# Delta-rule attention and two MoE layers on one core: the first two groups' diagonal Gram blocks are copied from the Gram product, the first join runs in halves, the inverses step by one product

## The chip, the cores and the metric

The kernel runs on one core of a Trainium2 chip. The metric is the device time of one execution in microseconds: 880.42 us, the median of three runs (880.21 to 883.84).

## The reference

Three layers run one after the other, in f32. The first is a delta-rule recurrence for 4 batches of 8 heads, 768 steps, head size 48; the second and third are feed-forward layers over the 3072 tokens that it makes.

```python
for t in range(S):                                   # k_n = k / (|k| + 1e-6)
    y[:, :, t] = einsum('bhd,bhde->bhe', q[:, :, t], state)
    v_old = einsum('bhde,bhd->bhe', state, kt)
    state = state + bt * einsum('bhd,bhe->bhde', kt, vt - v_old)
h = x @ w_in;  e = exp(h - max(h));  solu = h * e / sum(e)        # x: y as (3072, 384)
x = (solu - mean(solu)) / sqrt(var(solu) + 1e-6) * g_ln @ w_out   # d_ff 1024
out = square(relu(x @ w2_in)) @ w2_out                            # d_ff 2048
```

## The kernel before, in words

The recurrence is cut into chunks of 64 steps. Inside a chunk the steps are solved together: the Gram matrix of the chunk's keys, below its diagonal and scaled by beta and the key norms, is inverted, and the chunk's values go through that inverse. A tile `t` (24 in all) holds one pair of chunks of four batch-head pairs on 128 partitions. Its 64x64 Gram matrix is handled as blocks of 32 columns (`HB`): two diagonal blocks, each of which is inverted for itself, and the block between them, with which the two inverses are joined.

Tiles come in groups of four (`G0`): group 0 is t = 0 to 3 (`T1` = 4), group 1 is t = 4 to 7 (`T2` = 8). The stages that the change touches:

- `e_mm(t)` (line 699) multiplies keys by queries and keys into two PSUM banks: 16 f32 products, which are 32 matmul instructions in the profile. `e_out(t)` copies the negated key part to `g` (for the first group to `g0`, which lies in the raw weight buffers `raw[2]` and `raw[3]`), masks the query part into `m`, and sends `g` to the DRAM scratch `gscr`. `load_tb` reads the off-diagonal half back as `g12`.
- `d_tile(t)` (line 779), for the first two groups alone, multiplies the keys a second time, 32 products of 32x32 (64 matmul instructions) a tile, so that the diagonal blocks lie in the PSUM tile `p_h` in the layout that the inversion wants. For later groups the inversion loads them from `gscr`.
- `norms` and `gammas` make the scale `gm` from beta and the norms of the keys (VectorE and GpSimd, then a small matmul, line 867, and ScalarE copies).
- `first` inverts group 0's diagonal blocks on VectorE: a transpose into `tu` (line 1042), four scaled products (1052), 14 steps of a product and a sum on blocks of 16 (1063 and 1074), two more products, two transposes (1101, 1106). `join` then joins the blocks of 16 with small matmuls: `mm1` over all 32 (line 1129), one VectorE operation (1134), then `mm2` and `mm3` in two halves (1151, 1157), and copies into `tr`.
- `turn_in` transposes group 1's diagonal blocks out of `p_h` (line 880), and `inversion(1)` inverts them on GpSimd, row by row: a scaling (916), a triangle (923), and for each of 30 rows a product (948) and a sum (963). From row 10 on the columns are cut in two parts that use two halves of the temporary, so that there are 51 products and 51 sums. Groups 2 to 5 go the same way later.
- `turn(g)` transposes an inverse into the tiles `tr` and `tu` (1214, 1212), after which `prep1`, `prep2` and `z` (1294, 1314, 1341) prepare a tile and the chain of the state (`a_mm`, `o_mm`) takes it.
- `load_w1i` and `load_w1o` bring the weights of the second layer by DMA and convert them on ScalarE and VectorE, with the lower part of `w_out` on GpSimd (437). On VectorE that starts behind `first`'s inverse (`after=first_inv`).

The main loop over `t` runs the chain for tile `t`, `e` for tile `t + 9`, and the second layer for tiles `t - 2` and `t - 3`; the third layer follows.

What sets the order is a planner: every operation is handed to `Plan.add` with an engine, an assumed cost, what it reads and writes, and a priority. `Plan.order` simulates the engines in 12 rounds and emits all operations in the order of the best round; each engine then runs its own in that order. `HOLD` is how long an engine is kept for a more urgent operation that is about to be ready. All DMAs are issued from SP's queue. `gate` makes every DMA that is handed to the planner after it wait, in the plan, for the scratch write of tile 3.

Of the kernel before, what the change touches and what calls it, by code (L numbers as in the profile page):

```python
# [123 lines left out]
class Plan:  # L124
# [11 lines left out]
    HOLD = {"pe": 0.0, "dve": 0.042, "act": 0.174, "pool": 0.0, "sp": 0.0, "x": 0.0}  # L136
# [138 lines left out]
def c_turn(n):  # L275
    return 0.07 + n * 1.95e-3
# [12 lines left out]
def tile_delta_moe_moe(  # L289
# [39 lines left out]
    gscr = [dpool.tile([P, 2, GS * NP, HB], F32, name=f"gscr{g}") for g in range(NG)]  # L329
# [41 lines left out]
    v.tensor_reduce(out=low16, in_=ibd[:, HB // 2 :], axis=AX.X, op=ALU.add, negate=True)  # L371
# [36 lines left out]
    ngm = ap_.tile([P, HB], F32, name="ngm")  # L408
# [17 lines left out]
    pool.memset(tr[:, :, :, HB:], 0.0)  # L426
    g0 = raw_all[:, NRAW - 2 :].bitcast(F32).rearrange("q a n u -> q (a n u)")
    g0 = g0.rearrange("q (t h s c) -> q t h s c", t=4, h=2, s=2 * NP)
# [20 lines left out]
    def load_w(src, n, prio, bank, keep=False):  # L449
# [13 lines left out]
        if src.dtype == F32:  # L463
# [8 lines left out]
            [kr, *(("A", "g0", x) for x in range(4) if kr == ("A", "raw", NRAW - 2 + x // 2))],  # L472
# [187 lines left out]
    def e_in(t):  # L660
        if t < 2:
            return kql_[t], [("A", "kql", t)]
        if 4 <= t < 7:
            x, k = (ez_[t - 4], ("ez", t - 4)) if t < 6 else (junk, ("junk",))
            return x.rearrange("q (i p c) -> q i p c", i=2, p=NP), [k]
        return kqe_[t % 2], [("A", "kqe", t % 2)]

    def e_banks(t):
        if t >= LA:
            return pu, ku  # L670
        return (
            ((p_h[:, 0:512], p_h[:, 512:]), (("h", 0), ("h", 1))),
            ((p_tr, p_x1), (("tr",), ("x1",))),
            (pu, ku),
            ((p_a, p_o), (("A", "a"), ("A", "o"))),
        )[t if t < T1 else (1 + (t - T1) % 2 * 2 if t < T2 else 2)]
# [25 lines left out]

    def e_out(t, prio):
# [7 lines left out]
        if t < T1:  # L711
            gt, kg = g0[:, tg].rearrange("q h (i p) c -> q h i p c", i=2), [("A", "g0", tg)]
        banks, kb = e_banks(t)
        for i in range(2):
            gp, kep = banks[i].rearrange("q (p c) -> q p c", p=NP), [kb[i]]
            add(
                "act",
                c_act(256),
                lambda i=i, gp=gp: act.mul(
                    gt[:, :, i].rearrange("q h p c -> q p h c"),  # L720
                    gp[:, :, C:P].rearrange("q p (h c) -> q p h c", h=2),
                    -1.0,
                ),
                kep,
                kg,
                prio + ev,
            )
# [16 lines left out]
            else:  # L744
# [9 lines left out]
                )  # L754
        return dma(
# [7 lines left out]

    def e_tile(t, prio):
        e_load(t, prio)
        fused(1.15, [e_mm(t)], prio)
        return e_out(t, prio)

    def d_tile(t, prio):
        kq, kkq = e_in(t)  # L770
        d = p_h.rearrange("q (s t c) -> q s t c", t=4, c=HB)[:, :, group(t)[1]]

        def mm():
            for i, p, h in both:
                f = heads[h]
                for e in range(2):
                    o = (h ^ i) * C + e * HB
                    k = kq[f, i, p, C + e * HB : C + e * HB + HB]
                    pe.matmul(d[o : o + HB, i * NP + p], k, k, start=True, stop=True)  # L779

        add("pe", 0.7, mm, [*kkq, *((*kkq[0], "in", h) for h in range(2))], [("h", 0), ("h", 1)], prio)
# [33 lines left out]
    def gammas(g, prio):  # L815
# [55 lines left out]
        if g == 1:  # L871
            add("act", c_act(HB), lambda: act.mul(ngm, gt, -1.0), [kgt], [("ngm",)], prio)

    last_inv = []

    def turn_in():
        add(
            "dve",
            c_turn(HB * HB),
            lambda: v.transpose(it_[1].rearrange("s r c -> s c r"), p_h.rearrange("r (s t c) -> r c t s", t=4, c=HB)),  # L880
            [("h", 0), ("h", 1)],
            [("A", "itr", 1, q) for q in range(4)] + [("A", "it", 1, q) for q in range(2)],
            PR["turn1"],
        )

    def inversion(g, en, prio):
# [3 lines left out]
        it, itmp = it_[g % 2], junk[:, 512:] if g == 1 else itmp_  # L890
        kgm, kic = ("A", "gm", g % 2), ("A", "itc", g % 2)
        kts = [("A", "it", g % 2, q) for q in range(2)]
        ktm = [("A", "itmp", g == 1, q) for q in range(2)]
        kj = [("junk",)] if g == 1 else []
# [16 lines left out]
        gc, kgc = (ngm, [("ngm",)]) if g == 1 else (gm, [kgm])  # L911
        gb = gc.unsqueeze(1).to_broadcast([P, HB, HB])
# [4 lines left out]
            [*kraws, *kgc],  # L917
            [*kts, kic, *kj],
# [18 lines left out]
        s1, half_ = 9, HB * HB // 4  # L937
        used, run, brk = [], 0.0, []
        for j in range(1, HB - 1):
            nr = HB - 1 - j  # L940
            for q, (c0, c1) in enumerate(((0, min(j, s1)), (s1, j))):
                w_ = c1 - c0
                if w_ <= 0:
                    continue
                tm = itmp[:, q * half_ : q * half_ + nr * w_].rearrange("p (r s) -> p r s", r=nr)
                mul = one(
                    nr * w_,
                    lambda tm=tm, j=j, nr=nr, w_=w_, c0=c0, c1=c1: eng.tensor_tensor(  # L948
                        out=tm,
                        in0=it[:, j + 1 :, j : j + 1].to_broadcast([P, nr, w_]),  # L950
                        in1=it[:, j : j + 1, c0:c1].to_broadcast([P, nr, w_]),
                        op=ALU.mult,
                    ),
                    [kts[q], kic],
                    [ktm[q]],
                    brk,
                    full=False,
                )
                if q == 0:
                    used = [*used[-1:], mul]  # L960
                last = one(
                    nr * w_,
                    lambda tm=tm, j=j, c0=c0, c1=c1: eng.tensor_tensor(  # L963
                        out=it[:, j + 1 :, c0:c1],
                        in0=it[:, j + 1 :, c0:c1],
                        in1=tm,
                        op=ALU.add,
                    ),
                    [ktm[q], *kj],
                    [kts[q]],  # L970
                    used[:-1] if q else (),
                )
                run += 2 * c_pool(nr * w_)
                if g == 1 and run > 0.75:

                    fn = lambda: pool.memset(idle, 0.0)
                    brk = [add("pool", 0.1, fn, (), [("idle",)], prio, after=[last])]
                    run = 0.0
# [16 lines left out]
    def first(prio):  # L995
# [3 lines left out]
        it, kit = it_[0], [("A", "it", 0, q) for q in range(2)]  # L999
        kgs = [("A", "kqe", 0), ("A", "kqe", 0, "in", 0), ("A", "kqe", 0, "in", 1)]  # L1000
        gs = kqe_[0].rearrange("q i p c -> q (i p c)").rearrange("q (s c) -> q s c", c=HB)
        kh = [("h", 0), ("h", 1)]
        x = xo.rearrange("q a b -> q (a b)")[:, 0:512].rearrange("q (b r c) -> q b r c", b=2, r=H2)
        kx = [("xo", c) for c in range(3)]
# [5 lines left out]
        def dve(n, fn, r, w, c=None):  # L1010
            return add("dve", c or c_dve(n) + 0.09, fn, r, w, prio)
# [6 lines left out]
                in_=gm.unsqueeze(1).to_broadcast([P, HB, HB]),  # L1018
# [3 lines left out]
                compare_op=ALU.is_gt,  # L1022
# [7 lines left out]
        add(  # L1030
            "act",
            c_act(HB * HB),
            lambda: act.copy(
                gs.rearrange("q (t s) c -> q s t c", t=4), p_h.rearrange("q (s t c) -> q s t c", t=4, c=HB)
            ),
            kh,
            kgs,
            prio,
        )
        dve(  # L1040
            0,
            lambda: v.transpose(tu.rearrange("s r c -> s c r"), p_h.rearrange("r (s t c) -> r c t s", t=4, c=HB)),
            kh,
# [3 lines left out]
        for o, ko in ((org, ku[:1]), (x, kx)):  # L1047
            for b in range(2):
# [3 lines left out]
                    lambda o=o, b=b, q=q: v.scalar_tensor_tensor(  # L1052
                        out=o[:, b], in0=tu[:, q, q], scalar=-1.0, in1=it[:, q, q], op0=ALU.mult, op1=ALU.mult
                    ),
                    [*ktu(), *kit],
# [25 lines left out]
        for b in range(2):  # L1081
# [7 lines left out]
                        in1=gm[:, q].unsqueeze(2).to_broadcast([P, H2, H2]),  # L1089
                        op=ALU.mult,  # L1090
                    ),
                    [*kx, kgm],
# [15 lines left out]
        def join():  # L1108

            add(  # L1110
                "pool",
                1.0,
                lambda: pool.tensor_copy(aj[:, :, H2:], ibd[:, H2:].unsqueeze(1).to_broadcast([P, HB, H2])),
                (),
                kit,
# [3 lines left out]
            a1 = p_h[:, 0:512].rearrange("q (s c) -> q s c", c=H2)  # L1119
# [5 lines left out]
            def mm1():  # L1125
                for s in range(HB):
                    for hb in range(4):
                        q, k = slice(hb * HB, hb * HB + HB), slice(hb * HB, hb * HB + H2)
                        pe.matmul(a1[q, s], gs[k, s], td[k, s], start=True, stop=True)

            add("pe", 2.0, mm1, [*kgs, *ktd], [("h", 0)], prio)
            dve(
                512,
                lambda: v.scalar_tensor_tensor(
                    out=aj[:, :, 0:H2],
# [858 lines left out]
```

## Time and profile before

| what | value |
|---|---|
| median of three runs | 880.42 us (880.21 to 883.84) |
| the profiled execution, device time | 886.9 us |
| its span (first to last instruction) | 885.2 us |
| TensorE busy | 808.7 us, 11016 matmuls |
| VectorE busy | 469.8 us |
| ScalarE busy | 448.3 us |
| GpSimd busy | 280.9 us |
| granted TensorE clock over the span | 0.976 of full speed |

The profile is that of one execution, and all durations below are from it. An engine is busy while one of its instructions runs; the idle time before an instruction is put down to what released it ("issue" where the profile shows nothing that the engine waited for). Matmul durations overlap, since matmuls are pipelined. The span begins with a stretch in which the first two groups are prepared, goes on to the main loop, and ends with the third layer.

### The profile page before, as it was taken

What the parts mean: (1) busy time and instruction counts of PE and PEld (TensorE: products, weight loads), DVE (VectorE), ACT (ScalarE), POOL (GpSimd) and SP (SyncE); (2) the same over time, 40 slices, a digit from 0 to 9 for tenths busy, and PEclk for the clock granted to TensorE, in tenths of its full rate; (3) what the DMA queues carried; (4) which work ended last, traced back from release to release, by engine and by line L of the source; (5) the groups of instructions that cost most, each with busy time, mean ns of one, the idle gap of its engine ahead of it and who ended that gap; (6) DMA issues with size and microseconds to landing.
All of it is one profiled execution on the core that took longest, in us unless ns stands there. A gap on an engine that the chain in (4) does not pass through costs nothing.

```text
span 885.2 us, 26110 instructions
## 1 busy us (share of the span) xinstructions
PE 808.7 (91%) x11016; PEld 752.2 (85%) x11016; DVE 469.8 (53%) x906; ACT 448.3 (51%) x1006; POOL 280.9 (32%) x729
## 2 busy tenths in 40 slices
PE   5537689999899999899999999999999999999997
PEld 4436568889787788778788999999999999999997
DVE  5387784564876775865746543343434343343332
ACT  2236686866567658476656444343434333343333
POOL 5387488979569569610000000000000000000000
PEclk9999879999798899999999999999999999999999
DMA  9844664553778465434144312020201002010101
GB/s 205 256 118 143 179 187 141 146 151 108 217 199 253 149 173 170 148 108 157 47 150 134 101 37 55 1 54 0 54 1 45 10 1 55 1 27 0 28 1 27
DMA packets 70053, 89.34 MB, mean 101 GB/s; under 512 B 23088, under 2 KB 54832, under 8 KB 69936
## 3 DMA queue, kind: packets, MB, share of 16 engines
q1 hardware_dynamic: 69936, 87.68, 34.4%
q8 instruction: 86, 1.41, 0.7%
q14 instruction: 31, 0.25, 0.1%
HBM read 65.64 MB, written 22.02 MB: 99 GB/s over the span
## 4 chain that ended last, share of the span: by engine, by line
PE 84%; DVE 4%; issue 4%; ACT 4%; DMA 3%; POOL 0%; SPq 0%; ACTq 0%; POOLq 0%
PE h L1716 22%; PE acc L1760 22%; PE p_h L1451 12%; PE p_x L1573 11%; PE p_u L1341 2%; PE p_a L1368 2%; PE p_u L699 2%; PE p_tr L1553 2%; PE p_o L1399 1%; PE p_a L1314 1%; PE p_a L1398 1%; PE p_a L1294 1%; DMA kqe<-in_kin_dram 1%; PE p_h L779 1%; DVE sc L1466 1%
## 5 line engine op out<-in xcount | busy, mean ns | idle before, releaser
L1737 DVE TENSOR_TENSOR xt<-xt 128x384 f32<-128x384 f32 x128 | 71.5, 559 | 162.5 <-ACT xt L1729 162.4
L1729 ACT ACTIVATE xt<-h 128x384 f32<-128x384 f32 x128 | 63.0, 492 | 166.8 <-PE h L1716 166.6
L1716 PE MATMUL h<-x1h,w2h 128*128 128x384 f32 x384 | 128.5, 335 | 0.8 <-ACT xt L1729 0.8
L1716 PE MATMUL h<-x1l,w2h 128*128 128x384 f32 x384 | 128.3, 334 | 0.0
L1716 PE MATMUL h<-x1h,w2l 128*128 128x384 f32 x384 | 128.3, 334 | 0.0
L1760 PE MATMUL acc<-woh,xh 128*128 128x384 f32 x258 | 86.3, 334 | 0.0
L1760 PE MATMUL acc<-woh,xl 128*128 128x384 f32 x258 | 86.2, 334 | 0.0
L1760 PE MATMUL acc<-wol,xh 128*128 128x384 f32 x258 | 86.2, 334 | 0.0
L1573 PE MATMUL p_x<-zh,wgh 128*128 128x256 f32 x288 | 84.1, 292 | 0.3 <-ACT xo L1587 0.3
L1573 PE MATMUL p_x<-zh,wgl 128*128 128x256 f32 x288 | 81.2, 282 | 0.0
L1573 PE MATMUL p_x<-zl,wgh 128*128 128x256 f32 x288 | 81.2, 282 | 0.0
L963 POOL TENSOR_TENSOR it<-it,itmp 128x85 f32<-128x85 f32 (+29 forms) x204 | 76.2, 399 | 2.4
L948 POOL TENSOR_TENSOR itmp<-it 128x85 f32<-128x85 f32 (+29 forms) x204 | 73.4, 385 | 2.4
L1716 PEld LDWEIGHTS h<-x1h,w2h 128*128 128x128 f32 x384 | 72.1, 188 | 1.1 <-ACT xt L1729 1.1
L1716 PEld LDWEIGHTS h<-x1l,w2h 128*128 128x128 f32 x384 | 72.1, 188 | 0.0
L1716 PEld LDWEIGHTS h<-x1h,w2l 128*128 128x128 f32 x384 | 72.1, 188 | 0.0
L437 DVE TENSOR_TENSOR xl<-xt,xh 128x384 fp32r<-128x384 f32 x86 | 48.0, 558 | 44.9 <-ACT xh L432 44.6
L432 ACT CAST xh<-xt 128x384 fp32r<-128x384 f32 x86 | 44.3, 515 | 46.3 <-DVE xt L1737 45.1
L1451 PE MATMUL p_h<-w1h,xh 128*128 128x512 f32 x144 | 64.0, 445 | 2.8 <-DVE xl L437 2.8
L1451 PE MATMUL p_h<-w1l,xh 128*128 128x512 f32 x144 | 59.7, 415 | 0.0
L1451 PE MATMUL p_h<-w1h,xl 128*128 128x512 f32 x144 | 59.6, 414 | 0.0
L1573 PEld LDWEIGHTS p_x<-zh,wgh 128*128 128x128 f32 x288 | 54.2, 188 | 2.7 <-ACT xo L1587 0.5
(233 smaller groups left out, 1950.1 us busy)
## 6 DMA issues: line engine op xcount, KB each, us to landing
kql<-in_kin_dram SPq DMA_DIRECT2D x22, 512.0 KB, 4.5
kqe<-in_kin_dram SPq DMA_DIRECT2D x38, 192.0 KB, 4.8
raw<-in_w2i_dram SPq DMA_DIRECT2D x12, 512.0 KB, 5.4
raw<-in_w2o_dram SPq DMA_DIRECT2D x16, 384.0 KB, 4.6
gscr<-g SPq DMA_DIRECT2D x20, 256.0 KB, 5.1
m<-in_ktok_dram SPq DMA_DIRECT2D x24, 192.0 KB, 3.8
vt<-in_vtok_dram SPq DMA_DIRECT2D x24, 192.0 KB, 4.5
x1scr<-xo SPq DMA_DIRECT2D x12, 384.0 KB, 2.6
```

The costliest lines, as they stand in the source:

```text
L432: add("act", c_act(n), lambda: act.copy(hi(), src()), r, [w[0]], prio)
L437: lambda: le.tensor_tensor(out=lo(), in0=src(), in1=hi().bitcast(F32), op=ALU.subtract),
L699: pe.matmul(gp[i][rows[h ^ i], p], kq[f, i, p, C:P], kq[f, i, p], start=True, stop=True)
L948: lambda tm=tm, j=j, nr=nr, w_=w_, c0=c0, c1=c1: eng.tensor_tensor(out=tm, in0=it[:, j + 1 :, j : j + 1].to_broadcast([P, nr, w_]), in1=it ...
L963: lambda tm=tm, j=j, c0=c0, c1=c1: eng.tensor_tensor(out=it[:, j + 1 :, c0:c1], in0=it[:, j + 1 :, c0:c1], in1=tm, op=ALU.add,),
L1341: pe.matmul(zp[i][rows[h], p].rearrange("q (j c) -> q j c", j=7), tb[r, i * NP + p], m[r, i, :, p], start=True, stop=True,)
L1451: pe.matmul(p_h[:, sl], xx[:, c], ww[:, c, sl], start=(c == 0 and k == 0), stop=(c == 2 and k == 2),)
L1573: pe.matmul(p_x1[:, 0 : 2 * P], ww[:, f, c * P : c * P + P], zz[:, f], start=(f == 0 and k == 0), stop=(f == 7 and k == 2),)
L1716: pe.matmul(late["h2", ih], late[ww][:, c, s], xx[:, c], start=(c == 0 and k == 0), stop=(c == 2 and k == 2),)
L1729: lambda: act.activation(out=rt, in_=late["h2", ih], func=AF.Relu),
L1737: lambda: v.tensor_tensor(out=gg, in0=rt, in1=rt, op=ALU.mult),
L1760: pe.matmul(late["acc", a], gg[:, a * P : a * P + P], late[ww][:, f], start=(f == 0 and k == 0), stop=(f == 15 and k == 2),)
```

## The change

The diff is cut to its core; what is left out are mostly changed buffer keys, that is, names by which the planner orders reads and writes.

- `d_tile` and `turn_in` are gone. `e_out` for t < 8 makes two ScalarE copies of 128 columns a bank in place of one of 256: one to the place of `g12` (`first_g`), one to the group's array of diagonal blocks `gd_` (in `junk` for group 0, in `raw[3]` for group 1). `own` then copies the odd blocks from the former into the latter, one part on ScalarE, one on GpSimd.
- Group 0 no longer goes through `gscr` in either direction; group 1 writes half as much and reads it back as before.
- `first` reads `gd_[0]`; its four products take `gm` itself, and the triangle comes in at the last products. The copy from `p_h` on ScalarE (line 1033) is gone. Tile 6 takes the buffer `kqe` and not `junk`.
- In `join`, `mm1` and the VectorE operation behind it run in halves, and the block of the identity is copied on ScalarE, not GpSimd.
- In `inversion`, each row is one product and one sum.
- The copy of `vt` to `R` for t = 0 goes to ScalarE; `gate` is no longer set; `HOLD` of GpSimd is 0.11.

```diff
-    HOLD = {... "pool": 0.0, ...}
+    HOLD = {... "pool": 0.11, ...}
...
+    def first_g(t):
+        if t < 2:
+            return g0[:, 2 * NP * t : 2 * NP * t + 2 * NP], ("A", "tb", 0, 0)
+        if t >= T1:
+            return g_[t % 2][:, 1].rearrange("q i p c -> q (i p) c"), ("A", "g", t % 2)
+        return g12_[t % 2], ("A", "g12", t % 2)
...
+            if t < T2:
+                b0, kb0 = first_g(t)
+                s0 = slice(i * NP, i * NP + NP)
+                ss = slice((2 * tg + i) * NP, (2 * tg + i + 1) * NP)
+                for h, to, kg_, ss in ((1, b0, [kb0], s0), (0, gd_[g], kgd_[g], ss)):
+                    add("act", c_act(128),
+                        lambda gp=gp, to=to, ss=ss, h=h: act.mul(to[:, ss], gp[:, :, C + h * HB : C + h * HB + HB], -1.0),
+                        kep, kg_, prio)
...
+    def own(t, prio):
+        g, tg = group(t)
+        b0, kb0 = first_g(t)
+        for h in range(2):
+            q, ss = slice((2 * h + 1) * HB, (2 * h + 2) * HB), slice(2 * NP * tg, 2 * NP * tg + 2 * NP)
+            add("pool" if h else "act", 0.35,
+                lambda q=q, fn=pool.tensor_copy if h else act.copy: fn(gd_[g][q, ss], b0[q]),
+                [kb0], [kgd_[g][h]], prio)
...
-            for q, (c0, c1) in enumerate(((0, min(j, s1)), (s1, j))):
...
+            tm = itmp[:, 0 : nr * j].rearrange("p (r s) -> p r s", r=nr)
+            one(nr * j, lambda ...: eng.tensor_tensor(out=tm,
+                    in0=it[:, j + 1 :, j : j + 1].to_broadcast([P, nr, j]),
+                    in1=it[:, j : j + 1, 0:j].to_broadcast([P, nr, j]), op=ALU.mult), ...)
+            last = one(nr * j, lambda ...: eng.tensor_tensor(
+                    out=it[:, j + 1 :, 0:j], in0=it[:, j + 1 :, 0:j], in1=tm, op=ALU.add), ktm, kts)
...
-        add("act", c_act(HB * HB), lambda: act.copy(gs..., p_h...), kh, kgs, prio)
-            lambda: v.transpose(tu.rearrange("s r c -> s c r"), p_h.rearrange("r (s t c) -> r c t s", t=4, c=HB)),
+            lambda: v.transpose(tu.rearrange("s r c -> s c r"), gs.rearrange("r s c -> r c s")),
...
-            add("pe", 2.0, mm1, [*kgs, *ktd], [("h", 0)], prio)
             for n in range(2):
+                def mm1(n=n):
+                    for s in range(16):
+                        for hb in range(4): ...
+                add("pe", 1.1, mm1, [*kgs, *ktd], [kh[n]], pr)
+                add("dve", c_dve(256) + 0.09, ...)
...
-            fn = lambda: v.tensor_copy(R, vp)
+            fn = lambda: (v.tensor_copy if t else act.copy)(R, vp)
...
     for t in range(T1):
-        d_tile(t, -66 + t)
+        own(t, -62)
     gammas(0, -61)
     join = first(-55)
     for t in range(T1, T2):
         e_tile(t, PR["e0"] + 0.1 * t)
+        own(t, PR["e0"] + 0.1 * t)
         norms(t, PR["n1"])
-    for t in range(T1, T2):
-        d_tile(t, PR["e0"] + 0.5)
-    turn_in()
+    add("dve", c_turn(HB * HB), lambda: v.transpose(it_[1]..., gd_[1]...), kgd_[1], ..., PR["turn1"])
     join()
     gammas(1, -56)
-    gate.append(wr)
     inversion(1, "pool", PR["inv1"])
...
-    load_tb(0, PR["prep0"])
     prep_z(0, PR["prep0"])
-    load_tb(1, PR["prep0"] + 2)
     prep_z(1, PR["prep0"] + 2, (1,))
...
-            if n2:
+            if n2 and t + 2 >= T1:
                 load_tb(t + 2, tp + PR["prep"])
```

## Rows read from the trace of the kernel before

**Rows 1.** Busy time by stretch: microseconds, busy (instructions) by engine, clock, DMA share, GB/s.
```profile
0.00:75.40 75.40, 35.05 (x1488) 30.13 (x1488) 44.04 (x117) 19.91 (x54) 49.08 (x126) 1.00 0.67 179
75.40:126.80 51.40, 39.13 (x866) 31.36 (x866) 39.54 (x81) 38.96 (x101) 31.45 (x98) 0.88 0.68 190
126.80:395.00 268.20, 254.65 (x5114) 220.05 (x5114) 175.46 (x341) 179.99 (x433) 198.00 (x506) 0.95 0.56 163
395.00:885.20 490.20, 479.83 (x3555) 470.64 (x3549) 210.72 (x369) 209.48 (x423) 2.38 (x3) 1.00 0.16 45
```

**Rows 2.** The chain that ended last, in order of time: start, microseconds, what.
```profile
17.65 1.13 PE p_h L779 x72
18.78 1.21 issue
...
21.52 4.66 issue
...
38.72 3.43 issue
...
95.80 4.74 issue
```

**Rows 3.** DMA queue of instructions, whole span: packets, MB, share of 16 engines.
```profile
q8 instruction: 86, 1.41, 0.7%
```

**Rows 4.** Timeline of VectorE: start, microseconds, line, operation, idle before and its releaser.
```profile
20.50 0.41 DVE L748 TENSOR_TENSOR m<-p_u,mask 128x256 f32<-128x256 f32 x1
...
27.86 1.98 DVE L1042 STREAM_TRANSPOSE tu<-p_h 128x1024 f32<-128x1024 f32 x1 [6.39 <-ACT kqe L1033]
...
42.60 1.93 DVE L880 STREAM_TRANSPOSE it<-p_h 128x1024 f32<-128x1024 f32 x1 [8.31 <-PE p_h L779]
...
48.94 2.49 DVE L1386 COPY r<-vt 128x384 f32<-128x384 f32 x1
...
55.44 1.11 DVE L1101 STREAM_TRANSPOSE itmp<-it 128x512 f32<-128x512 f32 x1
```

**Rows 5.** Timeline of TensorE, the join and the first tile behind it.
```profile
56.60 2.95 PE L1129 MATMUL p_h<-itmp,kqe 16*32 16x16 f32 x205 [8.10 <-DVE itmp L1101]
...
62.53 1.28 PE L1151 MATMUL p_u<-it,tu 32*32 32x32 f32 x76 [0.94 <-DVE it L1134]
...
75.42 1.28 PE L1341 MATMUL p_u<-m,tr 64*64 64x112 f32 x11 [0.54 <-ACT tr L1327]
```

**Rows 6.** Timeline of ScalarE: two copies out of PSUM.
```profile
17.95 0.38 ACT L719 ACTIVATE raw<-p_o 128x256 f32<-128x256 f32 x1
...
73.74 0.27 ACT L1300 COPY ys<-p_a 128x128 f32<-128x128 f32 x1 [1.78 <-PE p_a L1294]
```

**Rows 7.** Instructions of line 1386: duration in ns, shortest, median, longest; first and last start.
```profile
L1386 DVE COPY r<-vt x2: 664/1578/2492, 48.9 to 267.0; 128x384 f32<-128x384 f32 x2
```

**Rows 8.** Timeline of GpSimd: inversion of group 1, then rows of a later one.
```profile
48.86 2.35 POOL L916 TENSOR_TENSOR it<-it,ngm 128x1024 f32<-128x1024 f32 x1
...
53.31 0.24 POOL L948 TENSOR_TENSOR junk<-it 128x30 f32<-128x30 f32 x1
...
94.64 1.00 POOL L437 TENSOR_TENSOR wgl<-wst,wgh 128x384 fp32r<-128x384 f32 x1 [11.81 <-ACT wgh L432]
...
118.09 1.92 POOL L988 TENSOR_TENSOR it<-it,gm 128x1024 f32<-128x1024 f32 x1
...
201.30 0.56 POOL L948 TENSOR_TENSOR itmp<-it 128x198 f32<-128x198 f32 x1
201.94 0.78 POOL L963 TENSOR_TENSOR it<-it,itmp 128x198 f32<-128x198 f32 x2
...
208.74 0.83 POOL L948 TENSOR_TENSOR itmp<-it 128x153 f32<-128x153 f32 x2
...
210.31 0.81 POOL L948 TENSOR_TENSOR itmp<-it 128x144 f32<-128x144 f32 x2
```

**Rows 9.** The chain that ended last between 56.6 and 75.4 us, its shares by line.
```profile
by line: issue 37.6%; PE p_u L1151 21.6%; PE p_h L1129 20.7%; PE p_h L1157 5.1%; ACT tr L1171 4.9%; DVE it L1134 4.1%; PE p_a L1294 3.3%; ACT ys L1300 1.4%; ACT tr L1327 1.4%
```

More of the change, by code (lines that the diff above doesn't have):

```diff
@@ L327, in bufs @@
         return [pool_.tile(shape, dt, name=f"{name}_{i}") for i in range(n)]
-    gscr = [dpool.tile([P, 2, GS * NP, HB], F32, name=f"gscr{g}") for g in range(NG)]
+    gscr = [dpool.tile([P, 2, GS * NP, HB], F32, name=f"gscr{g}") for g in range(1, NG)]
+    gscr = [None, *gscr]
     x1scr = [dpool.tile([P, 3, 2 * P], F32, name=f"x1scr{i}") for i in range(NT // 2)]
@@ L471, in load_w @@
             (),
-            [kr, *(("A", "g0", x) for x in range(4) if kr == ("A", "raw", NRAW - 2 + x // 2))],
+            [kr],
             prio - 1,
@@ L767, in e_tile @@
         return e_out(t, prio)
[L769 to L781, printed above, removed]
     def norms(t, prio, after=()):
@@ L935, in inversion @@
         )
-        s1, half_ = 9, HB * HB // 4
-        used, run, brk = [], 0.0, []
+        run, brk = 0.0, []
         for j in range(1, HB - 1):
             nr = HB - 1 - j
-            for q, (c0, c1) in enumerate(((0, min(j, s1)), (s1, j))):
[L942 to L978, printed above, removed]
@@ new lines, in inversion @@
+            tm = itmp[:, 0 : nr * j].rearrange("p (r s) -> p r s", r=nr)
+            one(
+                nr * j,
+                lambda tm=tm, j=j, nr=nr: eng.tensor_tensor(
+                    out=tm,
+                    in0=it[:, j + 1 :, j : j + 1].to_broadcast([P, nr, j]),
+                    in1=it[:, j : j + 1, 0:j].to_broadcast([P, nr, j]),
+                    op=ALU.mult,
+                ),
+                [*kts, kic],
+                ktm,
+                brk,
+                full=False,
+            )
@@ new lines, in inversion @@
+            last = one(
+                nr * j,
+                lambda tm=tm, j=j: eng.tensor_tensor(
+                    out=it[:, j + 1 :, 0:j], in0=it[:, j + 1 :, 0:j], in1=tm, op=ALU.add
+                ),
+                ktm,
+                kts,
+            )
+            run += 2 * c_pool(nr * j)
+            if g == 1 and run > 0.75:
+                fn = lambda: pool.memset(idle, 0.0)
+                brk = [add("pool", 0.1, fn, (), [("idle",)], prio, after=[last])]
+                run = 0.0
@@ L1029, in first @@
         add("pool", 0.3, lambda: pool.memset(it[:, H2:, 0:H2], 0.0), (), kit, prio)
[L1030 to L1039, printed above, removed]
-        dve(
-            0,
-            lambda: v.transpose(tu.rearrange("s r c -> s c r"), p_h.rearrange("r (s t c) -> r c t s", t=4, c=HB)),
-            kh,
+        dve(
+            0,
+            lambda: v.transpose(tu.rearrange("s r c -> s c r"), gs.rearrange("r s c -> r c s")),
+            kgs,
             ktu(),
@@ L1110, in join @@
             add(
-                "pool",
-                1.0,
-                lambda: pool.tensor_copy(aj[:, :, H2:], ibd[:, H2:].unsqueeze(1).to_broadcast([P, HB, H2])),
+                "act",
+                0.55,
+                lambda: act.copy(aj[:, :, H2:], ibd[:, H2:].unsqueeze(1).to_broadcast([P, HB, H2])),
                 (),
-                kit,
+                [kit[1]],
                 prio,
             )
-            a1 = p_h[:, 0:512].rearrange("q (s c) -> q s c", c=H2)
+            a1 = [p_h[:, i * 512 : i * 512 + 256].rearrange("q (s c) -> q s c", c=H2) for i in range(2)]
             f_, k_ = [z.rearrange("q (s c) -> q s c", c=HB) for z in p_u], ku
@@ L1159, in mm3 @@
                             )
[L1161 to L1163 removed]
+                ka = [kit[1], kit[2 + n]]
+                add("pe", 1.1, mm2, [*ktu(hs=[n]), *ka], [k_[n]], pr)
+                add("pe", 0.6, mm3, [*ktu(hs=[n]), *ka], [ku_[n]], pr)
                 sl = slice(2 + 2 * n, 4 + 2 * n)
@@ L1203, in cols @@
             return tr[q, s0 : s0 + 4, :, o : o + HB].rearrange("q t s c -> q (t s) c")
+        if g == 1 and not lower:
+            add(
+                "pool",
+                0.6,
+                lambda: pool.memset(tr[:, 0, :, HB:], 0.0),
+                (),
+                [("A", "tb", 0, k) for k in (*range(5), *kup)],
+                prio - 20,
+            )
         cs = [slice(c, c + HB // 4) for c in range(0, HB, HB // 4)]
@@ L1810, in tile_delta_moe_moe @@
         e_tile(t, PR["e0"] + 0.1 * t)
+        own(t, PR["e0"] + 0.1 * t)
         norms(t, PR["n1"])
-    for t in range(T1, T2):
-        d_tile(t, PR["e0"] + 0.5)
-    turn_in()
+    add(
+        "dve",
+        c_turn(HB * HB),
+        lambda: v.transpose(it_[1].rearrange("s r c -> s c r"), gd_[1].rearrange("r s c -> r c s")),
+        kgd_[1],
+        [("A", "itr", 1, q) for q in range(4)] + [("A", "it", 1, q) for q in range(2)],
+        PR["turn1"],
+    )
     join()
     gammas(1, -56)
-    gate.append(wr)
     inversion(1, "pool", PR["inv1"])
```

173 lines of the change are left out of this document (94 added, 79 removed).

## The prediction

> **What bounds the kernel now.** I read busy time by stretch first [rows 1]. From 395 us on TensorE is busy for 479.83 of 490.20 us, from 126.8 to 395 for 254.65 of 268.20: no edit of the change touches that work, and little idle time is left in it. In the first 75.4 us, though, TensorE is busy for 35.05, VectorE for 44.04, ScalarE for 19.91 and GpSimd for 49.08 us: nothing is full, so a chain of waits sets this stretch, and all that the change edits lies here or feeds tile 4 soon after. What is saved here should come off the end almost whole.
>
> Second, the chain that ended last, in order of time [rows 2]. Its largest pieces in the first 50 us are stalls of TensorE marked "issue", in which it waited for nothing that the profile shows: 1.21 us at 18.78, 4.66 at 21.52, 3.43 at 38.72, all beside the small products of `d_tile`; a later one is 4.74 at 95.80. The queue of instructions moved 1.41 MB in 86 packets [rows 3], that is 16.4 KB a packet; the 11016 matmuls and as many weight loads are 22032 instructions, 256 a packet. I read the stalls as TensorE waiting for its own next packet of 128 matmuls with their loads: where products are tiny, it eats code faster than code comes.
>
> [...]
>
> Third, VectorE's timeline, which carries group 0's inverse [rows 4]. The inverse starts at 27.86, behind 6.39 us of idle time, since `p_h` was finished late. At 42.60 `turn_in`'s transpose stands in the middle of it, having waited 8.31 us for the `d_tile` of group 1, and the inverse's steps queue behind it. At 48.94 a copy to `R` takes 2.49 us. At 55.44 comes the transpose that feeds the join, which TensorE starts at 56.60; tile 0's `z` product follows at 75.42 [rows 5].
>
> **The change part by part.** *The second Gram product goes.* `d_tile` was 8 tiles x 64 = 512 of the 1488 matmuls before 75.4 us, four packets of code. What the inverse now waits for is ScalarE's copies. The last copy of tile 3 ended at 17.95 + 0.38 = 18.33 [rows 6]. A copy of 128 columns was 0.27 us, one of 256 was 0.38 [rows 6], so two small ones for a large one add 0.16 a bank: 0.3 for tile 3's two banks, and about 0.4 for its `own` copies: 19.1. But VectorE is busy with masks and the scale until 20.50 + 0.41 = 20.91 [rows 4]. So the transpose moves from 27.86 to 20.9: **-7.0**. Bounds: 19.1 if VectorE's order leaves a gap (-8.8); 21.5 if all of ScalarE's extra work for the group (8 x 0.16 + 4 x 0.38 = 2.8) and a last hand-over of 0.4 stand in a row (-6.4). `gm` needs the 8 matmuls of line 867; they no longer stand behind `d_tile`, and the first stall came only after tiles 0 to 3 (4 x 32) and 72 of `d_tile`'s [rows 2], 200 matmuls, so the four products find it ready.
>
> *`turn_in`'s wait.* The transpose of group 1 now needs tiles 4 to 7 copied. TensorE has 128 matmuls for them, directly behind the first 136; at most one packet boundary lies in that, so they should be done near 27 us, while VectorE's inverse runs to 35. **-8.3**; if the planner puts the transpose early, some 2 us of the wait stay. Its own 1.93 us stays.
>
> *The copy to `R`.* It took 2.49 us, where its other instance took 0.66 [rows 7], beside GpSimd's scaling of 2.35 at 48.86 [rows 8]; on ScalarE, idle there, it leaves this chain: **-2.5**.
>
> [...]
>
> *The join in halves.* TensorE stood 0.94 us before `mm2` for the VectorE operation [rows 5]. Now the second half of `mm1` can run under the first half's: **-0.9**. If the planner sets `mm2`'s first half directly behind `mm1`'s first, 128 matmuls less stand ahead, 2.95 x 128/205 = 1.8 us more; I don't count on it, since a free TensorE takes what is ready, and that is `mm1`'s second half. The copy of the identity on ScalarE costs nothing while ScalarE is idle; if it isn't, 0.6.
>
> The sum for tile 0: 7.0 + 8.3 + 2.5 + 0.9 = 18.7 us; `z` at 56.7 in place of 75.4.
>
> *Inverses by one product.* In the split form, row 14 (153 + 85 columns) takes 210.31 - 208.74 = 1.57 us [rows 8]; its two products overlap. For one product: 0.24 us at 30 columns, 0.56 at 198 [rows 8], so 1.9 ns a column, 0.64 at 238, and 201.94 - 201.86 = 0.08 between dependent ones; twice that is 1.43. So 0.14 at best in each of 21 rows, less in the short ones: 2 us a group, nothing like the 40% of instructions that go. For groups 2 to 5 it is worth nothing at the end, since TensorE sets that stretch.
>
> *What tile 4 waits for.* Group 1's inversion ran from 48.86 to 118.09 + 1.92, with an idle 11.81 us in it for the weights [rows 8]. Its start was held by `turn_in` like VectorE and gains 7.0 + 8.3 = 15.3, less eight new GpSimd copies (256 columns on 32 partitions; by its products of 0.24 to 0.56 an estimate of 0.4 each, 3.2), plus 2 for its length: 14.1. The 11.8 us of idle time are slack for that, and the wait itself moves with the main chain, 18.7. The end moves between 14.1 and 18.7; I take **17.5** for the whole.
>
> *DMAs.* Group 0's scratch writes (4 x 256 KB), half of group 1's (4 x 128 KB) and two loads of 128 KB go: 1.8 of the 179 GB/s x 75.4 us = 13.5 MB [rows 1]. The weights, no longer gated, may be issued before tiles 6 and 7, whose buffers come free late. The same DMA time without 13% in 57 us is a share of 0.76 where 0.67 was: not full. I cost it at nothing; if code packets queue behind the weights, it is the third rival.
>
> So the profiled execution should go from 886.9 to 869.4 (885.2 span and 1.7 around it). It lies 6.5 above the median of the runs, and I assume the same after: 880.4 - 17.5 = **863 us**.
>
> **The rivals.** *GpSimd becomes the bound at tile 4.* If its masks for tile 7 and the copies of `own` hold it 3 us more, and the single products, each waiting for the one before, save nothing, group 1's inverse gains 15.3 - 3.2 - 3 = 9.1: 871. For it: GpSimd is the busiest engine of the first stretch [rows 1]. Against: the 11.8 us of slack.
>
> *The stalls are not code, or don't go with it.* Then the start and `turn_in` stay put but for the matmuls' own time, and the copy, the join and some 1.5 us are what is left: 2.5 + 0.9 + 1.5 = 5: 875. Against: packets of 256 instructions and stalls that sit in runs of tiny products.
>
> *Code packets wait behind the weights (slower).* In the join, 37.6% of 18.8 us, 7.1 us, are already "issue" [rows 9], over five packets. From the join to 126.8 there are twelve (640 and 866 matmuls). The gain of 17.5 is gone when each waits 1.5 us longer; at 2 more, well under the 4.66 and 4.74 seen, 24 are lost: 887. For it: the gate goes, and the loads get denser. Against: fewer bytes in all, and 0.68 of DMA share in that stretch [rows 1].
>
> *More than counted.* The stall of 4.74 at 95.80 falls elsewhere and the halves give their 1.8: 17.5 + 6.5 = 24: 856.
>
> **How the numbers follow.** The forecast has 0.60 (its own range, by the bounds of its terms, 857 to 869), GpSimd 0.17, stalls that stay 0.08, more than counted 0.08, code behind weights 0.07. A new order of all engines adds some scatter, which I put into the ends: 850 to 877. Half a per cent, 4.4 us, is about what can be told from no change. Only the slower rival lies above 885: slower 0.07; between, 0.05, from a milder form of it and of the stalls that stay; faster 0.88.
>
> **What would show it.** Right: 10504 matmuls; no stall of 3 to 5 us before 30 us; the inverse's transpose near 21; no idle time of several microseconds on VectorE inside the inverse; `mm1` near 38, tile 0's `z` near 57, and the main loop the same shape moved left. Wrong: `z` early but tile 4 late (GpSimd); the join longer than 19 us with more "issue" (code); or a gain that dies after 126.8, which would say that the main loop was not TensorE's.

## The result, and the profile after

The median after is 869.44 us (868.05 to 871.15) against 880.88 before (880.21 to 883.84), four runs each: a ratio of 0.9865, with a 95% interval from 0.9836 to 0.9893, and a gain of 11.4 us. The profiled execution went from 886.9 to 871.15 us, 15.75 less, its span from 885.2 to 869.4. Forecast were 863.0, that is a gain of 17.5, and 869.4 for the profiled execution.

Busy time by stretch of the kernel after (columns as in [rows 1]); the first two stretches end at tile 0's `z` and where [rows 1] end theirs, the last row runs to the end of a stretch used below.

```profile
0.00:61.15 61.15, 29.54 (x1041) 25.70 (x1041) 43.72 (x118) 26.34 (x84) 46.32 (x110) 0.66 0.69 188
61.15:126.80 65.65, 56.82 (x1358) 46.46 (x1352) 51.89 (x105) 53.81 (x134) 47.73 (x104) 0.80 0.72 202
126.80:395.00 268.20, 249.02 (x5005) 216.71 (x5005) 174.90 (x336) 177.50 (x426) 164.60 (x310) 0.96 0.54 161
...
0.00:186.00 186.00, 142.17 (x3402) 121.30 (x3403) 124.75 (x276) 117.03 (x305) 139.34 (x301) 0.80 0.62 170
```

The first stretch is 14.3 us shorter than in [rows 1], with 5.5 us less of TensorE's work. The queue of instructions of the kernel after, four packets fewer than in [rows 3]:

```profile
q8 instruction: 82, 1.34, 0.7%
```

VectorE's timeline of the kernel after, for [rows 4]: the inverse from its transpose (1040) to those that feed the join.

```profile
18.80 1.94 DVE L1040 STREAM_TRANSPOSE tu<-junk 128x1024 f32<-128x1024 f32 x1
...
23.86 0.43 DVE L1050 TENSOR_TENSOR p_u<-tu,gm 128x256 f32<-128x256 f32 x1 [2.67 <-ACT gm L904]
24.21 1.47 DVE L1050 TENSOR_TENSOR xo<-tu,gm 128x256 f32<-128x256 f32 x1
...
37.83 1.07 DVE L1102 STREAM_TRANSPOSE itmp<-it 128x512 f32<-128x512 f32 x1
38.98 2.07 DVE L1831 STREAM_TRANSPOSE it<-raw 128x1024 f32<-128x1024 f32 x1
40.94 1.90 DVE L1107 STREAM_TRANSPOSE tu<-it 128x1024 f32<-128x1024 f32 x1
43.34 0.46 DVE L1140 SCALAR_TENSOR_TENSOR it<-p_h,low,ibd 128x256 f32<-128x256 f32 x1
```

The transpose starts 9.06 us earlier, then stands 2.67 for `gm`; inside the inverse no wait of several microseconds and no copy to `R` are left (line 1401 is on ScalarE, 0.51 us). TensorE's join, for [rows 5] (1134 is `mm1`, 1157 and 1163 `mm2` and `mm3`, 1309 and 1329 `prep1` and `prep2`, 1356 `z`):

```profile
38.95 1.91 PE L1134 MATMUL p_h<-itmp,junk 16*32 16x16 f32 x128 [1.70 <-DVE itmp L1102]
43.94 0.92 PE L1163 MATMUL p_h<-tu,it 32*32 32x32 f32 x53 [3.08 <-DVE it L1140]
...
46.40 0.21 PE L1134 MATMUL p_h<-itmp,junk 16*32 16x16 f32 x1
...
48.17 1.68 PE L1134 MATMUL p_h<-itmp,junk 16*32 16x16 f32 x111 [1.26 <-issue]
...
52.45 0.38 PE L1309 MATMUL p_a<-tr 32*32 32x32 f32 x12 [2.31 <-issue]
...
56.17 0.48 PE L1157 MATMUL p_u<-it,tu 32*32 32x32 f32 x19 [1.80 <-issue]
...
61.15 1.13 PE L1356 MATMUL p_u<-m,tr 64*64 64x112 f32 x12
```

The join starts 17.65 us earlier and takes 22.2 us where it took 18.8. ScalarE's timeline of the kernel after has the copy (`tuc`) that frees `mm1`'s second half:

```profile
45.34 0.35 ACT L1188 COPY itmp<-p_h 128x256 f32<-128x256 f32 x1
```

GpSimd's, for [rows 8]: group 1's inversion (936 to 997), then a row of 238 columns in a later one.

```profile
41.89 2.35 POOL L936 TENSOR_TENSOR it<-it,gm 128x1024 f32<-128x1024 f32 x1
...
92.06 1.91 POOL L997 TENSOR_TENSOR it<-it,gm 128x1024 f32<-128x1024 f32 x1
...
130.15 0.62 POOL L963 TENSOR_TENSOR itmp<-it 128x238 f32<-128x238 f32 x1
130.85 0.65 POOL L976 TENSOR_TENSOR it<-it,itmp 128x238 f32<-128x238 f32 x1
131.58 0.61 POOL L963 TENSOR_TENSOR itmp<-it 128x240 f32<-128x240 f32 x1
```

The chain of waits after, for [rows 2]: in front of the join no "issue" piece above 0.75 us is left; the longest one now is this.

```profile
126.14 3.96 issue
```

### The profile page after: what moved, and what is told of

It is laid out like the page before. It is cut to its first block, busy times and chain, and to the rows that moved or that the text cites. A ratio compares the mean times of both kernels' runs of the same rounds, so it can differ in the third digit from the quotient of the medians.

```text
span 869.4 us, 24895 instructions
## 1 busy us (share of the span) xinstructions
PE 800.3 (92%) x10504; PEld 747.3 (86%) x10504; DVE 469.4 (54%) x906; ACT 453.0 (52%) x1030; POOL 259.5 (30%) x523
## 4 chain that ended last, share of the span: by engine, by line
PE 82%; ACT 5%; DMA 5%; DVE 4%; issue 3%; POOL 1%; SPq 0%; ACTq 0%; DVEq 0%; POOLq 0%
PE h L1731 23%; PE acc L1775 22%; PE p_x L1588 12%; PE p_h L1466 11%; PE p_a L1383 2%; PE p_tr L1568 2%; PE p_u L703 2%; PE p_u L1356 2%; DMA m<-in_ktok_dram 2%; PE p_o L1414 1%; ACT xt L1438 1%; PE p_a L1309 1%; DVE sc L1481 1%; PE p_a L1329 1%; PE p_a L1413 1%
## 5 line engine op out<-in xcount | busy, mean ns | idle before, releaser
L1731 PEld LDWEIGHTS h<-x1h,w2h 128*128 128x128 f32 x384 | 72.1, 188 | 0.0
L976 POOL TENSOR_TENSOR it<-it,itmp 128x30 f32<-128x30 f32 (+14 forms) x120 | 62.6, 521 | 8.5
L963 POOL TENSOR_TENSOR itmp<-it 128x30 f32<-128x30 f32 (+14 forms) x120 | 58.4, 486 | 8.6
```

What stands on the lines that cost most here:

```text
L963: lambda tm=tm, j=j, nr=nr: eng.tensor_tensor(out=tm, in0=it[:, j + 1 :, j : j + 1].to_broadcast([P, nr, j]), in1=it[:, j : j + 1, 0:j].to ...
L976: lambda tm=tm, j=j: eng.tensor_tensor(out=it[:, j + 1 :, 0:j], in0=it[:, j + 1 :, 0:j], in1=tm, op=ALU.add),
L1731: pe.matmul(late["h2", ih], late[ww][:, c, s], xx[:, c], start=(c == 0 and k == 0), stop=(c == 2 and k == 2),)
```

## The experiments

Kernels of one set ran on one chip beside the kernel before, whose medians in the three sets were 879.85, 878.25 and 878.45 us, with single runs from 871.1 to 886.8. Ratios are to before, with 95% intervals.

**Set 1. Is it code?** `b_again` and `a_again` are before and after unchanged. `b_nod` is before without most of the second Gram product:

```diff
                 for e in range(2):
+                    if (i, p, h, e) != (0, 0, 0, 0):
+                        continue
```

`a_all` is after with four moves in the emitted order: group 1's transpose behind the first 1140, group 0's `gm` product ahead of tile 4's `e`, tile 0's `z` ahead of tile 1's `prep1` (with the join's last copy ahead of tile 1's `ys`), the loads of tiles 6 and 7 ahead of the weights.

b_again: 

> The kernel before, unchanged, profiled once more. The first profiled execution took 886.9 us, 6.0 more than the median of the runs. If that was the scatter of one execution (what I hold now), this profile lands near 881 and the difference of some 6 us lies in one stretch that can be named (a stall, a stretch at the lower granted clock). Rival: profiling itself costs 6 us in this kernel, and this one is near 887 again.

b_nod: 

> The kernel before with d_tile cut to 1 of its 32 products a tile (496 matmuls fewer in all); waits, copies and every engine's order stay, and the diagonal blocks are not computed. Theory (the 'issue' stalls are TensorE waiting for code, 128 matmuls a packet): nearly four packets go, VectorE's transpose moves from 27.9 to about 21, its wait of 8.3 before the second transpose goes, tile 0's z comes some 15 us earlier (near 60), time about 866. Rival (the stalls are something else): only the matmuls' own time goes, some 6 us of TensorE and 2 to 3 at the end; stalls of 3 to 5 us before 45 us stay; about 878.

a_again: 

> The changed kernel, unchanged: a better interval and a second profile. Expected 869.4, ratio 0.987; tile 0's z near 61 and the main loop as in the first profile to 1 or 2 us. Rival: the profiled executions of both kernels scatter by some 6 us, then this one may lie anywhere from 866 to 873.

a_all: 

> The changed kernel with its planned order kept but for four moves: turn_in's transpose behind the first half's VectorE operation of the join; group 0's scale matmul ahead of tiles 4 and 5; tile 0's z ahead of tile 1's first two products (with one ScalarE copy); the loads of tiles 6 and 7 ahead of the first weights. Theory (these four places are where the chain lost what I had counted): 2.0 + 2.5 + 1.3 us earlier at tile 0's z, near 55.5, and 4 to 6 us less in all, 864. Rival (the main loop is held by weights, scale and inversion, not by tile 0): z as early, but the time within 1 us of 869.4.

Measured: `b_again` 878.53 us, profiled, `z` at 72.1. So a profile adds nothing like 6 us; the first one of before was a long execution of a kernel that scatters. Of the 8.4 us by which its span is longer, 3.3 had gone by tile 0's `z`, where a stall of 4.66 us was 2.90 in `b_again`, and 6.7 by tile 4's, where the one of 4.74 was 1.60. Its join and tile 0's `z`, for [rows 5]:

```profile
54.43 2.96 PE L1129 MATMUL p_h<-itmp,kqe 16*32 16x16 f32 x205 [8.07 <-DVE itmp L1101]
...
72.14 2.73 PE L1341 MATMUL p_u<-m,tr 64*64 64x112 f32 x32 [0.54 <-ACT tr L1327]
```

`a_again` 867.01, 0.9873 (0.9826 to 0.9920). `b_nod` 869.96, 0.9886 (0.9831 to 0.9941): taking 496 small products out, and nothing else, gives 9.9 us where the whole change gives 12.8 on the same chip, and the two intervals overlap for the most part. VectorE's transpose came at 21.31, as expected. TensorE's timeline of `b_nod` at the join's start and tile 0's `z`:

```profile
43.89 2.74 PE L1131 MATMUL p_h<-itmp,kqe 16*32 16x16 f32 x189 [8.09 <-DVE itmp L1103]
...
64.72 2.23 PE L1343 MATMUL p_u<-m,tr 64*64 64x112 f32 x32 [0.35 <-ACT tr L1329]
```

Its `z`, expected near 60, is 3.6 us later than after's, yet its span is 870.3 against 869.4. `a_all` has `z` at 59.4, where 55.5 was expected, and a median of 872.5, 0.9936 (0.9901 to 0.9970): earlier and not better.

**Set 2. The products put back, the other parts undone.** `a_dum` adds 512 small products to after, `a_few` eight wide ones, in the same places:

```diff
+            for _ in range(4 if t in (3, 7) else 0):       # a_dum
+                for i, p, h in both:
+                    for e in range(2):
+                        o = (h ^ i) * C + e * HB
+                        k = kq[heads[h], i, p, C + e * HB : C + e * HB + HB]
+                        pe.matmul(gp[i][o : o + HB, p, 0:HB], k, k, start=True, stop=True)
...
+            for n in range(4 if t in (3, 7) else 0):       # a_few
+                i, h = n % 2, n // 2
+                pe.matmul(banks[i][rows[h ^ i]], kq[heads[h], i, 0, C:P], kq[heads[h], i, 0:4], start=True, stop=True)
             for i, p, h in both:
```

`a_split` issues each product and each sum of a row in the column parts `(0, 9), (9, j)` again; `a_load` is the last of `a_all`'s moves alone.

a_dum: 

> The kernel after with 512 products of 32x32 put back on TensorE: 256 ahead of tile 3's e products and 256 ahead of tile 7's, into the bank that these then overwrite; every engine's order is as in the kernel after. Theory (code): the products bring four instruction packets back, and TensorE waits for them in front: some 12 us of waits put down to "issue" before 45 us (before: 1.21, 4.66, 2.71, 3.43), tile 0's z from 61 to 72-76, the end 8 to 12 us later than the kernel after, near 877. Rival (work): only TensorE's time for them counts, about 1.2 us for 95, 7 us in all and half of it under waits: z near 65, end +3, the same as the run with a few wide products. Rival (absorbed): z is late and the end is within 2 us of the kernel after.

a_few: 

> The kernel after with eight products of 512 columns in the places where the run beside it has 512 small ones: as much TensorE time or more (the 128-column products of e take 0.42 us, two at a time), hardly any code. Theory (code): no new wait put down to "issue", tile 0's z within 3 us of 61, the median within 0.3% of the kernel after. Rival (work): as late as the run with 512 small products.

a_split: 

> The kernel after with the GpSimd inversions' steps from the tenth on in two products and two sums again, as before, in the same places of every engine's order. The steps of a group should take some 7 us longer again (37.4 against 30.2 us). Theory (TensorE's idle time and work set the end, GpSimd does not): the median is within 0.3% of the kernel after. Rival (GpSimd bound before tile 4): tile 4's z 5 to 7 us later and the end 4 to 7 us later, near 872.

a_load: 

> The kernel after with the loads of tiles 6 and 7 put ahead of the first weight load on the DMA queue; nothing else moves. The wait of 4.66 us for kqe before tile 6's e products should go. Theory (the end follows from TensorE's idle time before tile 8's z, 43.7 us): if no later wait takes it over, the idle time falls by 4 and the end by 3 to 4, to 863-864. Rival (the wait passes to group 1's gamma turn or to the four transposes ahead of the join): idle time as before and the median within 0.3% of the kernel after.

Measured: `a_dum` 875.68 us, 0.9979 (0.9946 to 1.0011): nearly all of the gain is gone; against `a_few`, on the same chip, it is 9.6 us, with intervals that lie apart. Its `z` is at 69.2, earlier than the 72 to 76 expected. It has 86 packets again, and TensorE's waits (in total, times, longest) show the stalls in the added products' line:

```profile
PE p_o L707 <- issue: 7.7, 2, 4.9
PE p_a L707 <- issue: 6.3, 2, 4.2
```

`a_few` 866.09, 0.9854 (0.9808 to 0.9901): no loss, 82 packets, no wait for "issue" ahead of the join, `z` at 61.8. Its products are 16 matmul instructions and some 4.2 us of TensorE's time, less than I expected, where the 512 are 6.57 us. So it is the number of instructions that costs, not most of TensorE's work. `a_split` 868.23, 0.9899 (0.9849 to 0.9950), `z` of tile 4 at 112.4 against 114.3: the inversions' form is worth nothing that shows at the end. `a_load` 869.0, 0.9909 (0.9873 to 0.9945): the wait for `kqe` is gone and stands whole at group 1's `gm` product (902), where after had 4.2:

```profile
PE p_o L902 <- ACT g L734: 9.9, 1, 9.9
```

**Set 3. Half the dose, the join, a better one.** `a_third` is after once more; `a_half` has only tile 7's 256 products (`4 if t == 7`); `a_turn` has the first of `a_all`'s moves alone, `a_fturn` that and `a_few`'s products.

a_third: 

> The kernel after once more, as what the other three of this set are read against: 867 to 869.

a_half: 

> The kernel after with only the 256 small products ahead of tile 7's e put back (512, in two lots, cost 8 us at tile 0's z and 4 to 8 at the end). Theory (code, by the packet): 84 instruction packets, two new waits put down to "issue" of some 4 us each ahead of 45 us; half of the cost at the end, 871 to 873. Rival (hidden at this place): tile 7's e waits for its load and the inverse on VectorE goes on meanwhile, so that z is within 1 us of 61 and the end as in the kernel after; then group 0's lot carried the cost, through the start of the inverse.

a_turn: 

> The kernel after with the transpose of group 1's blocks (2.07 us on VectorE between td and tu) put behind the first half's scalar_tensor_tensor; nothing else moves. Theory for the join's miss: the transpose in the middle delays tu and so mm3, which waited 3.08 us for VectorE; without it tile 0's z comes 2 us earlier, at 59, and GpSimd's inversion starts some 4 us later. At the end: within 0.3% of the kernel after, since TensorE's idle time ahead of tile 8's z stays near 43 us. Rival: the end follows z, 2 us earlier.

a_fturn: 

> The same move, with the eight products of 512 columns ahead of tiles 3 and 7, whose kernel showed the shortest profiled execution (861.9 span: no wait for code at 126 and in the loop, 4.0 and 2.9 to 3.6 us in the kernel after). If that wait depends on where the packets' borders fall, it stays away here too, and the time is 3 to 5 us under the kernel after, 863 to 865; if that was chance, 867 to 869.

Measured: `a_third` 868.85, 0.9902 (0.9867 to 0.9938). `a_half` 874.19, 0.9952 (0.9921 to 0.9983), two waits of 5.2 us together in the added line, `z` at 67.6: a loss for half the dose too, by medians 5.3 us, where the whole dose cost 6 to 9 against the three sets of runs of after; its interval overlaps that of `a_third`, so the loss itself rests on the medians and on `z`, and whether it is half stays open. `a_turn` 869.36, 0.9912 (0.9874 to 0.9950), `z` at 61.7, no gain. Its TensorE timeline says why:

```profile
41.52 0.92 PE L1164 MATMUL p_h<-tu,it 32*32 32x32 f32 x53 [0.95 <-DVE it L1141]
...
48.69 1.90 PE L1135 MATMUL p_h<-itmp,junk 16*32 16x16 f32 x128 [4.00 <-ACT itmp L1189]
```

`mm3` comes 2.4 us earlier, and `mm1`'s second half then waits 4.00 for the copy of line 1189. `a_fturn` 862.21 us, 0.9825 (0.9779 to 0.9871), is the shortest of all, 6.6 us under `a_third` by medians; the two intervals just overlap. All its waits for "issue" of half a microsecond or more:

```profile
PE p_u L1162 <- issue: 2.9, 2, 1.5
PE p_h L1168 <- issue: 1.8, 2, 1.5
PE p_h L1139 <- issue: 1.1, 1, 1.1
PE p_a L1388 <- issue: 0.7, 1, 0.7
PE p_x L1593 <- issue: 0.5, 1, 0.5
```

They sum to 7.0 us, where after has 14.3 (3.96 of it at 126), `a_third` 11.5, before 25.4 and `b_again` 20.4. Sixteen more matmuls, at 128 a packet (10504 in 82 after), moved the packets' borders against the code; that this is the cause was not isolated. `a_few` has only 7.3 us of such waits too, so they don't set `a_fturn` apart from it, and 869.36 (`a_turn`) and 866.09 (`a_few`) give no sign that either edit alone does all of it.

## Why the prediction was right, and where it was not

**The stalls were code: right.** Products taken out of before give nearly the whole gain, put back into after they take it away, and two thirds of their TensorE time in 16 instructions cost nothing. Four packets are 12.0 us of stalls in before (1.21 + 4.66 + 3.43 in [rows 2], and 2.71 at 36.23 in tile 7's `e`), 10.5 in `b_again`, 14.0 in `a_dum`. The traces show the packets too: every wait for "issue" of half a microsecond or more, 11 in before, 7 in after and 12 in `a_dum`, ends 1.2 to 1.7 us behind the end of a packet of the instruction queue. Most packets go with no such wait, 75 of before's 86; in the runs of small products there are long ones, 4.66 us in before's `d_tile` and 4.9 at the longest in `a_dum`.

**The inverse up to the join: near in sum, by luck in part, and not in its terms.** Predicted were 17.8 us up to `mm1` (7.0 + 8.3 + 2.5), measured 17.65; but against `b_again`, the same kernel, it is 54.43 - 38.95 = 15.48. The start gained 9.06, beyond its bound of 8.8 (6.90 against `b_again`, whose transpose starts at 25.70). In it is a gain that no term had: TensorE's first product, which waits for a load, starts at 4.80 where it started at 6.24 (4.57 to 5.43 in every kernel with after's order, 6.11 to 6.30 with before's). The hand-over of 0.4 in the start's other bound was my estimate: after's last copy of `own` ended at 18.57, and the transpose started at 18.80. `gm`, which I found ready since no stall lay before it, came 2.67 late, because TensorE ran its matmuls (line 901, at 23.25) behind tiles 4 and 5, and tile 4 waited for its load:

```profile
19.63 0.47 PE L703 MATMUL p_tr<-ez 48*64 48x128 f32 x1 [1.47 <-DMA ez<-in_kin_dram]
```

The transpose of group 1 left the inverse altogether, and with it its own 1.93 us. The copy to `R` did go, with its 2.49 us. In `b_nod`, where it stays on VectorE, it took 2.48 us at 36.23, beside GpSimd's scaling from 36.16 to 38.51; in after, a product of 1.47 us at 24.21 (the other three 0.43 to 0.73) lies beside GpSimd's triangle (line 1024) from 23.97 to 25.42. They ended 0.20 and 0.26 us behind the GpSimd instruction beside them (38.71 and 25.68), as the copy did in before, 0.22 behind (51.43 against 51.21). In after it is another VectorE instruction that is long, by some 0.8 us; what makes it so was not tested.

**"The join in halves: -0.9": wrong, +3.4.** I had `mm1`'s second half run under the first half's VectorE operation. It cannot: it is declared to read both halves of `td`, and the `tuc` copy behind the first half's `mm3` writes the first one.

```python
add("pe", 1.1, mm1, [*kgs, *ktd], [kh[n]], pr)      # reads ktd[0] and ktd[1], for either n
...
lambda n=n: act.copy(tuc[:, 8 * n : 8 * n + 8], u_[n][:, 0:8]), [ku_[n]], [ktd[n]], pr
```

So it started at 46.40, behind the copy's end at 45.69, after TensorE had stood 3.08 us for VectorE; moving the transpose only moved that wait (`a_turn`). Its products touch the other half alone, so narrower keys should allow what I assumed; that was not tried. Tile 1's `prep1` and `prep2`, 64 matmuls, also stand ahead of tile 0's `z` now, and the join's "issue" is hardly less (the three in the rows above and 0.92 at 59.63, 6.3 us; 7.1 by [rows 9]). So `z` came at 61.15, not 56.7 (the join of `b_again` took 17.7 us, which makes it +4.5): a lead of 14.3 us over before and of 11.0 over `b_again`, where 18.7 was the sum.

**"Inverses by one product": right.** A row of 238 columns was to go from 1.57 to 1.43; it takes 131.58 - 130.15 = 1.43. The sum of busy time falls more (the products of a split row overlap: at 208.74 in before 0.49 and 0.40 us in 0.83), which misled me in `a_split`'s expectation, not in the prediction.

**"I take 17.5 for the whole": 11.4 by medians, and not by the way I thought.** The 15.75 between the two profiled executions is no measure of it, as the first was a long one; by medians the change gained 11.4 us here, 12.8 in `a_again` and 9.6 in `a_third`. The term had been read from the rows of that long execution, and I took the lead at the chain as what comes off the end. The lead was 14.3 us at tile 0's `z`, 29.2 at tile 5's and 13.8 at tile 8's; over `b_again` it was 11.0, 22.7 (124.7 against 147.4) and 7.3 (186.2 against 193.5). The starts of tile 5's and tile 8's `z`, before and after:

```profile
153.88 0.30 PE L1341 MATMUL p_u<-m,tr 64*64 64x112 f32 x1
...
199.98 1.00 PE L1341 MATMUL p_u<-m,tr 64*64 64x112 f32 x32
```
```profile
124.67 0.30 PE L1356 MATMUL p_u<-m,tr 64*64 64x112 f32 x1
...
186.21 1.00 PE L1356 MATMUL p_u<-m,tr 64*64 64x112 f32 x32
```

Group 1's inversion, which was to gain 14.1, ended 26.0 us earlier (93.97 against 120.01; against `b_again`'s 113.37 it is 19.4). It started only 7.0 earlier where 15.3 was counted, but took 52.1 us where it had taken 71.2, 11.81 of them idle for the weights. `b_nod`, with 14.5 at tile 5, has 14.2 at tile 8 (against `b_again` 8.0 and 7.7). What differs is how much of the second layer TensorE did on the way. Its products (first of its output, line 1588, then of its input, line 1466; TensorE's busy time and number, clock, DMA share, GB/s) up to tile 5's `z` and from there to tile 8's, after:

```profile
0.00:124.70 124.70, 3.29 (x24) 0.73 0.70 194
...
0.00:124.70 124.70, 16.06 (x54) 0.73 0.70 194
124.70:186.20 61.50, 20.20 (x72) 0.94 0.46 122
```

The same in `b_nod` (lines 1575 and 1453):

```profile
0.00:139.40 139.40, 6.65 (x48) 0.94 0.69 195
...
0.00:139.40 139.40, 23.24 (x72) 0.94 0.69 195
139.40:185.80 46.40, 14.13 (x54) 1.00 0.56 142
```

The order of after puts the chain ahead of the second layer; that work is still to be done, and by tile 8 both kernels have done nearly the same (168 and 126 of these products after, 156 and 126 in `b_nod`). What counts is TensorE's idle time. Busy by stretch, before, `b_again`, `b_nod` and `a_fturn`, each up to about tile 8's `z`:

```profile
0.00:200.00 200.00, 146.64 (x3906) 124.03 (x3906) 124.68 (x274) 111.23 (x281) 143.16 (x374) 0.96 0.61 169
```
```profile
0.00:193.50 193.50, 146.13 (x3907) 123.67 (x3907) 125.12 (x274) 111.43 (x282) 143.53 (x374) 0.92 0.63 175
```
```profile
0.00:186.00 186.00, 143.79 (x3415) 119.64 (x3419) 125.40 (x274) 111.73 (x282) 143.43 (x375) 0.95 0.66 181
```
```profile
0.00:183.00 183.00, 144.41 (x3419) 123.31 (x3419) 124.83 (x276) 116.95 (x305) 139.92 (x301) 0.94 0.63 173
```

Idle are 53.4 us before (47.4 in `b_again`), 42.2 in `b_nod`, 43.8 after, 38.6 in `a_fturn`, 48.5 in `a_all` in spite of its early `z`. From before to after, 9.5 us of idle and 4.5 of work make the 14 at tile 8, and 2 more come behind it; from `b_again` it is 3.5 and 3.8, and next to nothing behind. So the direct copies, the join and the inversions gave the chain a lead that TensorE's order turned into waits further on (4.72 us for group 2's scale at 101, the 3.96 at 126), and the instructions that went are nearly the whole gain, as far as the runs can tell: 7.7 us at tile 8 in `b_nod`, 7.3 after, both against `b_again`. The step of the prediction that failed is the one from the chain to the end ("should come off the end almost whole").

**"It lies 6.5 above the median of the runs, and I assume the same after": wrong,** and the larger part of the miss. After's profiled execution lies 1.7 above its median, `b_again`'s 1.3 under that of its set. What lay above was this execution's own scatter, not an offset: the 17.5, read from its rows, has that scatter in it, and the difference of the medians has not. That is 4.8 of the 6.4 us by which 863.0 is short. The rest is the 1.75 of the profiled execution, and that this one came so near its 869.4 is luck in so far as the rows were those of a long execution.

**The rivals.** GpSimd was no bound at tile 4: in `a_split` the split rows took 6.5 us more of its time between 41 and 94 us (46.04 against 39.55), and group 1's inversion was no longer for it (40.90 to 92.93, against 41.89 to 93.97). Code behind weights did not come; the join's "issue" stayed as it was. "More than counted" did not come either: the stall at 95.80 went, and 3.96 at 126 and 2.91 at 218 came. A gain that dies after 126.8 was named as what would say that the main loop is not TensorE's; most of a lead did die there, for another reason: the loop is TensorE's, and a lead of the chain is none of TensorE's.

## What to carry to other kernels

Where a queue of instructions feeds runs of tiny matmuls, count instructions, not flops: here 512 of 32x32 were worth nearly the whole gain (9.6 us between `a_dum` and `a_few`). Where an engine's work is fixed and it sets the later stretch, price an early edit by the idle time that it takes from that engine, not by how much earlier a chain arrives. Before counting on an overlap, read the declared buffers of both halves; and take an offset of one profiled execution for scatter until a second one shows it.

## What was not expected of the hardware

The clock granted in the first 61 us did not matter: it was 0.66 of full speed after, 1.00 in `a_third`, the same program, with `z` at 61.15 and 61.9. `a_third`, its busy time in this stretch:

```profile
0.00:61.00 61.00, 29.61 (x1008) 25.09 (x1008) 42.91 (x117) 25.51 (x82) 46.10 (x109) 1.00 0.72 188
```

Later it does. From tile 20's `z` to the second tile of the third layer, with 3.9 us idle each time, `a_few` took 129.7 us with no time at a granted clock of 0.50 of full speed, after 131.9 (378.7 to 510.6) with 5.5 us of it, `a_third` 132.0 with 5.8, `a_turn` 134.5 with 11.4, `a_half` 134.8 with 12.1: some 0.4 us for each. Part of the scatter between executions is this.

A stall can be longer than its packet's transfer. In `a_dum` the packets at 15.75 and 22.44 took 1.37 and 1.08 us; TensorE stood from 15.82 to 18.57 and from 20.12 to 25.04. It ran on some 1.5 us after each transfer's end, and the second time it had stopped 2.3 us before the transfer began. In before, likewise, it stood from 21.52 to 26.18, with a packet of 0.97 us at 23.89. What sets when a packet is sent was not tested; in before and `b_again`, the same program, the stall at line 1398 was 4.74 and 1.60 us.
